# Two chunks of a batch in one load, two tokens in each partition, for two of four batches of an RWKV-5 and squared-ReLU kernel

## The chip, the cores and the metric

The kernel runs on one core of one Trainium2 chip. The core has five queues of instructions that run beside each other: TensorE (PE in the profile; its weight loads are shown as PEld), VectorE (DVE), ScalarE (ACT), GpSimd (POOL) and SyncE (SP), which here only issues transfers. The metric is the device time of one execution in microseconds, taken as the median of several runs.

## The reference

An attention with a decaying state, per batch (4) and head (8, each of 48 columns), over 768 tokens, and then a two-layer network with a squared ReLU over all 3072 tokens:

```
for t in range(S):                       # S = 768
    cur = einsum('bhd,bhe->bhde', u * k[t], v[t])
    y[t] = einsum('bhd,bhde->bhe', r[t], state + cur)
    state = w * state + einsum('bhd,bhe->bhde', k[t], v[t])
x = y.transpose(0, 2, 1, 3).reshape(3072, 384)
h = maximum(x @ w_in, 0)                 # 384 -> 2048
out = (h * h) @ w_out                    # 2048 -> 384
```

r, k and v are float32 arrays of [4, 8, 768, 48], so a token of one head is a run of 192 bytes in memory. w_in and w_out are float32 and are turned to bf16 on the way in.

## The kernel before, in words

**Units.** Tokens are cut into chunks of 128. A unit is one chunk of one batch; there are 24, and unit i is chunk i // 4 of batch i % 4. A unit has 128 tokens in the 128 partitions and all eight heads in the columns. Units 0 to 3 (the first chunks) start from an empty state; each later one needs the state that the unit four before it left.

**Steps of one unit, in the attention.** `ld` loads r, k or v of a unit (L387). `kh` and `rh` scale k and r by powers of w (L424, L430) and write bf16. `T` transposes the scaled pair on PE (L454) and `Tc` copies the result from PSUM to SBUF; for later units `XB`, a transposing transfer, does both. `A` computes the 128 x 128 table of k against r for each head, in eight matmuls (L476). `Bm` multiplies it by a triangular mask on DVE (L501). `Y` multiplies that table by v and adds what the state gives (L509). `U` is the new part of the state, k against v (L536); `S0`, `ts` and `S` decay and sum it. `P0`, `P1`, `du` and `dv` compute the term with u (r times k, times u, summed per head, times v). `vb` turns v to bf16. `xs` adds Y and dv. `X` transposes the sum on PE and `xTc` copies it out; for later units `xX` does it by transfer.

**The network.** Units are put into groups. `F1.g.s` is a piece of the first layer for group g (L587): it fills one PSUM bank with 512 columns. For a group of one unit these are four pieces of 128 hidden columns by 128 tokens, so twelve 128-column matmuls; for a group of two, two pieces by 256 tokens, so six 256-column matmuls. `re` takes the ReLU of the bank (on ACT or DVE) and `sq` squares it. `F2.i.f.4` adds four of sixteen hidden pieces of the second layer for unit i (L615). `os` copies the sum out of PSUM and `out` stores it. The last unit's second layer is done in two column halves (`F2c`).

**Weights.** `lW.0.s` loads a float32 piece of w_in of 384 KB through SP into one of six staging tiles (`st`), and `cW` turns it to bf16 on ACT, DVE or POOL (L403). `W` loads and converts in one transfer issued by POOL (L416), which is done for one piece of w_in and for all four of w_out. A piece of w_in serves two hidden pieces, so F1 step s of a group of two needs piece s, and of a group of one pieces 2s and 2s+1.

**What sets the order.** Nothing is scheduled by the compiler. The string ORDER at the top (L24) lists every step with its engine (P, A, D, G for POOL, S for SP) and its buffers after the slashes: `A.0:P/4/5` is step A of unit 0 on PE into PSUM banks 4 and 5. Each engine runs its steps strictly in that order, so a step that waits holds all that stand behind it on its engine. There are eight PSUM banks; a step that writes one waits until its last reader is done. `Z` steps are matmuls on the identity whose result nobody reads.

**The start.** Small tables come first: w is spread to all partitions by a shuffle (`shw`), u by another (`shu`, L329), then ACT takes logarithms and powers (`logw`, `WkQ`, `WtQ`, `WkS`, `WtS`). u's own load is issued by SP (L323). POOL fills the identity and one mask (L257).

Of the kernel before, what the change touches and what calls it, by code (L numbers as in the profile page):

```python
# [11 lines left out]
ALU = mybir.AluOpType  # L12
# [14 lines left out]
A.0:P/4/5 ld.k.2:S/3 WtS:A P1.3:G kh.1:D/2 lW.0.1:S/0 rh.1:D/2 T.1:P/6 Tc.1:A/1 A.1:P/7/3 Tc.3:A/2 A.3:P/6/2 ld.v.0:S/0  # L27
ld.v.3:S/1 vb.3:G/0 kh.2:D/3 U.3:P/0 du.3:D/1 P0.1:D/2 P1.1:D dv.3:G rh.2:D/3 du.1:D/2 lW.0.5:S/1 cW.0.5:A T.2:P/1 cW.0.1:D
Bm.0.1:D/0 Bm.1.0:D/1 vb.0:A/1 Tc.2:A/3 Bm.0.0:D/2 Y.0:P/5 U.0:P/7 Bm.3.1:D/3 A.2:P/1/4 Bm.3.0:D/4 ld.v.1:S/2 Y.3:P/2 dv.0:G
xs.0:D/0 lW.0.0:S/2 X.0:P/6 cW.0.0:A vb.1:G/2 Bm.1.1:D/5 xs.3:D/1 Y.1:P/5 xTc.0:D/0 X.3:P/3 xTc.3:A/0 P0.2:G/3 P1.2:G  # L30
du.2:D/3 dv.1:G F1.0.0:P/2 re.0.0:A/0 xs.1:D/2 X.1:P/6 lW.0.4:S/3 cW.0.4:G F1.0.2:P/3 re.0.2:A/1 W.0.2:G ld.v.2:S/3 dv.2:G
vb.2:A/3 lW.0.6:S/4 lW.0.7:S/5 Bm.2.0:D/2 W.1.0:G xTc.1:D/1 F1.1.2:P/2 F1.1.0:P/5 Bm.2.1:D/0 Y.2:P/3 re.1.2:A/2 lW.0.3:S/1
wc:S cW.0.6:D U.2:P/1 ld.r.4:S/4 cW.0.7:D F1.1.3:P/6 re.1.0:A/3 sq.1.0:A0/0 re.1.3:A/4 xs.2:D/3 WLcol:A X.2:P/4 xTc.2:D/0
sq.0.0:D2/1 F1.0.3:P/2 cW.0.3:G F1.2.0:P/5 re.0.3:A/5 F1.2.3:P/6 re.2.0:D/3 sq.2.0:A0/2 F1.2.1:P/3 re.2.1:D/0 F1.0.1:P/4
sq.2.1:D2/3 ld.k.4:S/4 WLm:G S0.0:D re.2.3:A/3 sq.2.3:A0/4 S0.2:D F1.2.7:P/2 re.2.7:A/0 W.1.1:G P0.4:D/4 F1.2.6:P/5 kh.4:G/4
F2.3.0.4:P/3 ld.k.5:S/5 F2.0.0.4:P/7 S0.3:D re.2.6:A/3 sq.2.6:A0/5 sq.1.2:D2/6 F1.1.1:P/6 rh.4:D/4 F2.1.0.4:P/1 F1.2.2:P/2
re.2.2:D/3 sq.0.3:A0/7 F1.2.5:P/0 W.1.2:G F2.2.0.4:P/5 re.0.1:D/2 re.1.1:A/5 sq.1.1:A0/8 ld.r.5:S/5 re.2.5:A/5 sq.2.5:A0/9
T.4:P/2 P1.4:D F1.2.4:P/4 Tc.4:A/4 F2.1.4.4:P/1 sq.2.2:D2/10 F2.2.4.4:P/5 U.1:P/6 F2.3.4.4:P/3 rh.5:G/5 kh.5:D/5 T.5:P/0
# [685 lines left out]
```

## Time and profile before

| What | Value |
|---|---|
| median of 3 runs | 173.31 us (173.05 to 173.64) |
| profiled execution | 174.07 us, of which span 172.3 us |
| PE busy | 161.7 us (94%) |
| DVE busy | 139.9 us (81%) |
| ACT busy | 104.5 us (61%) |
| POOL busy | 88.2 us (51%) |
| granted TensorE clock, mean | 0.98 |
| moved by transfers | 29.13 MB in 105,588 packets, 98,008 of them under 512 B |

How to read the profile: the span runs from the first to the last instruction of the profiled execution. Busy time of an engine counts the time in which at least one of its instructions ran; matmuls are pipelined, their ends are modelled, and a busy PE need not be at its peak. In a group of instructions the columns are line, engine, operation, output and inputs by the program's names, shapes and count, then busy time in us and the mean of one instruction in ns, then the idle time of the engine just before them and what ended it. A row of the timeline has start and length in us, and in brackets the idle time before it and the releaser. The chain of waits goes back from the last instruction to what released it; its rows have start, length and what ran. An `x6` is the number of instructions in a row.

### The profile page before, as it was taken

What the parts mean: (1) busy time and instruction counts of PE and PEld (TensorE: products, weight loads), DVE (VectorE), ACT (ScalarE), POOL (GpSimd) and SP (SyncE); (2) the same over time, 40 slices, a digit from 0 to 9 for tenths busy, and PEclk for the clock granted to TensorE, in tenths of its full rate; (3) what the DMA queues carried; (4) which work ended last, traced back from release to release, by engine and by line L of the source; (5) the groups of instructions that cost most, each with busy time, mean ns of one, the idle gap of its engine ahead of it and who ended that gap; (6) DMA issues with size and microseconds to landing.
All of it is one profiled execution on the core that took longest, in us unless ns stands there. A gap on an engine that the chain in (4) does not pass through costs nothing.

```text
span 172.3 us, 4337 instructions
## 1 busy us (share of the span) xinstructions
PE 161.7 (94%) x1691; PEld 121.6 (71%) x1691; DVE 139.9 (81%) x272; ACT 104.5 (61%) x187; POOL 88.2 (51%) x105
## 2 busy tenths in 40 slices
PE   3976899999999997999999999999999999999993
PEld 1445788776787776777687696886686786878772
DVE  5599887569999996788999899779989889682731
ACT  3475477694599485467569276595596454553740
POOL 5425967215857497998339402879922872000000
PEclk9995699999999999999999999999999999999999
DMA  5999999999697998999999997999595963130322
GB/s 99 218 230 257 330 211 192 202 147 224 112 204 153 209 205 190 231 194 183 238 176 211 185 206 140 230 159 234 132 130 107 127 136 98 44 93 0 141 91 91
DMA packets 105588, 29.13 MB, mean 169 GB/s; under 512 B 98008, under 2 KB 105568, under 8 KB 105568
## 3 DMA queue, kind: packets, MB, share of 16 engines
q1 hardware_dynamic: 103672, 26.95, 76.2%
q0 software_dynamic: 1744, 1.77, 6.8%
q8 instruction: 13, 0.21, 0.5%
q10 hardware_dynamic: 152, 0.14, 0.2%
q14 instruction: 7, 0.06, 0.1%
HBM read 20.46 MB, written 4.72 MB: 146 GB/s over the span
## 4 chain that ended last, share of the span: by engine, by line
PE 71%; SPq 10%; DMA 7%; ACT 5%; DVE 2%; issue 2%; POOL 1%; POOLq 0%; ACTq 0%
PE bank L622 31%; PE bank L594 29%; SPq L388 5%; SPq L396 4%; DMA st<-in_moe_w_in_dram 4%; DMA ldv<-in_v_dram 3%; PE bank L494 3%; ACT hr L602 2%; PE bank L531 2%; ACT hq L609 2%; PE bank L527 2%; PE bank L552 2%; PE bank L636 2%; PE bank L578 1%; DVE S0W L567 1%
## 5 line engine op out<-in xcount | busy, mean ns | idle before, releaser
L594 PE MATMUL bank<-xT,W 128*128 128x256 bf16 (+1 forms) x624 | 71.2, 266 | 0.4 <-DVE W L288 0.3
L622 PE MATMUL bank<-W,hq 128*128 128x384 bf16 x368 | 68.5, 326 | 0.3 <-DVE S0W L567 0.3
L594 PEld LDWEIGHTS <-W 128*128 128x128 bf16 x624 | 56.1, 99 | 9.0 <-DVE W L288 0.5
L602 ACT ACTIVATE hr<-bank 128x512 bf16<-128x512 f32 x70 | 40.6, 593 | 27.5 <-PE bank L594 26.8
L609 ACT ACTIVATE hq<-hr 128x512 bf16<-128x512 bf16 x72 | 43.6, 626 | 7.3 <-DVE hr L604 6.1
L622 PEld LDWEIGHTS <-hq 128*128 128x128 bf16 x368 | 33.9, 98 | 19.2 <-ACT hr L602 0.5
L507 DVE TENSOR_TENSOR Bm<-bank,maskJT 128x512 bf16<-128x512 f32 x48 | 31.1, 678 | 0.6 <-PE bank L494 0.6
L604 DVE TENSOR_SCALAR hr<-bank 128x512 bf16<-128x512 f32 x26 | 17.6, 686 | 11.7 <-PE bank L594 9.7
L441 POOL TENSOR_TENSOR P<-P,ub 128x384 f32<-128x384 f32 x14 | 15.0, 1072 | 16.2 <-DVE P L437 15.9
L434 POOL TENSOR_TENSOR rk<-ldr,Wt 128x384 bf16<-128x384 f32 x13 | 13.8, 1063 | 7.8 <-DMA ldr<-in_r_dram 7.8
L449 POOL TENSOR_TENSOR dv<-ldv,du 128x384 f32<-128x384 f32 x16 | 13.9, 878 | 2.8 <-DVE du L444 2.8
L560 DVE TENSOR_TENSOR xs<-bank,dv 128x384 bf16<-128x384 f32 x24 | 13.1, 552 | 2.0 <-PE bank L531 0.9
L444 DVE TENSOR_REDUCE du<-P 128x8 f32<-128x384 f32 x24 | 12.9, 545 | 1.6 <-POOL P L441 1.3
L286 ACT COPY os<-bank 128x384 f32<-128x384 f32 x13 | 5.9, 487 | 13.4 <-PE bank L622 13.4
L573 POOL TENSOR_TENSOR S0W<-ts,WLm 128x384 bf16<-128x384 f32 x9 | 9.4, 1053 | 8.7 <-DVE ts L570 8.6
L428 POOL TENSOR_TENSOR rk<-ldk,Wkhat 128x384 bf16<-128x384 f32 x12 | 12.8, 1076 | 2.0 <-DMA ldk<-in_k_dram 1.9
L531 PE MATMUL bank<-vb,Bm 128*128 128x48 bf16 x192 | 11.6, 187 | 1.5 <-DVE Bm L507 0.9
L613 DVE TENSOR_TENSOR hq<-hr 128x512 bf16<-128x512 bf16 x24 | 12.4, 523 | 0.3
L288 POOL CAST vb<-ldv 128x384 bf16<-128x384 f32 x10 | 6.1, 606 | 12.7 <-DMA ldv<-in_v_dram 11.5
L437 POOL TENSOR_TENSOR P<-ldr,ldk 128x384 f32<-128x384 f32 x10 | 10.6, 1066 | 3.4 <-DMA ldr<-in_r_dram 3.4
L531 PEld LDWEIGHTS <-Bm 128*128 128x128 bf16 x192 | 9.9, 99 | 2.6 <-DVE Bm L507 1.7
L288 DVE COPY os<-bank 128x384 f32<-128x384 f32 (+2 forms) x12 | 6.2, 518 | 6.0 <-PE bank L622 2.7
(67 smaller groups left out, 163.7 us busy)
## 6 DMA issues: line engine op xcount, KB each, us to landing
ldr<-in_r_dram SPq DMA_DIRECT2D x24, 192.0 KB, 4.0
ldk<-in_k_dram SPq DMA_DIRECT2D x24, 192.0 KB, 3.7
ldv<-in_v_dram SPq DMA_DIRECT2D x24, 192.0 KB, 4.2
out_dram<-os SPq DMA_DIRECT2D x23, 192.0 KB, 2.3
st<-in_moe_w_in_dram SPq DMA_DIRECT2D x7, 384.0 KB, 5.6
W<-in_moe_w_out_dram POOLq DMA_DIRECT2D x4, 384.0 KB, 7.2
rkT<-rk SPq DMA_TRANSPOSE x17, 3.7
W<-in_moe_w_in_dram POOLq DMA_DIRECT2D x1, 192.0 KB, 5.1
```

The lines of the kernel that those rows point to most:

```text
L434: e.tensor_mul(scaled("r", i), loaded("r", i), early("WtQ") if i < EARLY else Wt2)
L441: e.tensor_mul(t, t, ub)
L444: e.tensor_reduce(dub[slot[f"dv{i}"]], P0b[slot[f"P{i}"]], axis=mybir.AxisListType.X, op=ALU.add)
L449: e.tensor_mul(dvb[slot[f"dv{i}"]], loaded("v", i), t)
L507: e.tensor_mul(o, a, mask_b)
L531: e.matmul(y[:, hc, D * h : D * (h + 1)], m[h][:, hc, :], vb[:, 2 * hc + h, :], start=(i < B), stop=True, skip_group_check=True,)
L560: e.tensor_add(xsb[slot[f"xs{i}"]].rearrange("p (a b) -> p a b", a=HP), heads(bank(f"bY{i}"), 2 * D), dvb[slot[f"dv{i}"]].rearrange("p (a ...
L594: e.matmul(hp[:, fi, :], W1[f // 2][:, c, 128 * (f % 2) : 128 * (f % 2 + 1)], xt[:, c, :], start=(c == 0), stop=(c == CCH - 1), skip_group ...
L602: e.activation(hr, hp, AF.Relu)
L604: e.tensor_scalar_max(hr, hp, 0.0)
L609: e.activation(hq, hr, AF.Square)
L622: e.matmul(bank(f"bO{i}")[:, 0:d_model], hqb[slot[f"hq{g},{f // m}"]][:, at : at + L], W2[f // 4][:, f % 4, :], start=(summed[i] == 1), st ...
```

## The change

The kernel takes two of the four batches (0 and 1, `DUO = 2`) out of the plain scheme for their first two chunks.

- **Loads.** `ldD.x.p` loads chunks 0 and 1 of batch p, 256 tokens, in one transfer of 384 KB into a staging tile: partition q holds tokens 2q and 2q+1, so a run in memory is two tokens, 384 bytes. Six such loads (k, r, v of two batches) replace twelve loads of 192 KB.
- **Units.** Units 0 and 1 are the even and odd tokens of those 256 of batch 0, units 2 and 3 those of batch 1. Partitions 0 to 63 are chunk 0 and partitions 64 to 127 are chunk 1. Units 4 to 7 are chunks 0 and 1 of batches 2 and 3; from unit 8 on the order is as before.
- **A in quarter tiles.** For the four new units `AD.t` computes the tables of both the even and the odd keys against unit t's queries, each within its own half of the partitions: 32 matmuls of 64 x 64. `BmD` masks them with one of two half masks, which POOL fills at the start (two fills and eight selects more).
- **Y in quarter tiles.** Y of such a unit sums over even and odd keys: 32 small matmuls, and four more that add, for the upper half of the partitions, the state that chunk 0 left. That state comes from new steps: `UC.p` on PE (eight matmuls on the lower half) and `SC.p` on ACT, two copies of 48 x 192 from PSUM into a table `carry`.
- **State.** U of a pair is computed once for 256 tokens (`U.1`, `U.3`, eight matmuls each), and decayed by the square of the old factor (`WL2`). So 18 U steps instead of 20, two of them double.
- **Powers of w.** Four new ones (`WkD`, `WtD`), since neighbouring tokens now differ in partition by a half.
- **Groups.** Twelve groups of two units instead of two groups of one and eleven of two.
- **Where work runs.** u's load moves from SP to POOL; the column of w comes from eight small matmuls (`wc`) instead of two transfers; weight casts move to ACT (6 of 7); seven `Z` steps instead of two; `sq` on DVE 36 instead of 24 times, on ACT 60 instead of 72. Staging tiles: 8 instead of 6.
- **Order.** ORDER is another one throughout. Its start is shown.

```
-GROUPS = [1, 1, 2, 2, 2, 2, 2, 2, 2, 2, 2, 2, 2]
-PAIRED = 0
-EARLY = 4
+GROUPS = [2, 2, 2, 2, 2, 2, 2, 2, 2, 2, 2, 2]
+DUO = 2
+EARLY = 6
...
-w:A ld.r.3:S/0 ld.k.0:S/0 ld.r.0:S/1 shw:D u:S P0.0:G/0 shu:D tab:A logw:A WkQ:A/0 WtQ:A/1 rh.0:D/0 ld.r.1:S/2 ld.k.3:S/1
-WkS:A rh.3:D/1 kh.3:D/1 Z.66.7:P T.3:P/2 ld.r.2:S/3 kh.0:D/0 ld.k.1:S/2 P1.0:G du.0:D/0 P0.3:D/1 T.0:P/3 Tc.0:A/0 Z.22.7:P
...
+ldD.k.0:S/0 w:A tab:A ldD.r.0:S/1 ldD.k.1:S/2 u:G ldD.r.1:S/3 ld.k.4:S/0 shw:D ld.r.4:S/0 logw:A ld.r.5:S/1 WtD.1:A/0
+Z.24.5:P wc:P/2 P0.0:D/0 P0.1:G/1 WtD.0:A/1 rh.1:D/0 ldD.v.1:S/4 WkD.1:A/3 rh.0:D/1 WLcol:A shu:D WkD.0:A/6 kh.3:D/2
+ld.k.5:S/1 WkQ:A/7 P1.1:G kh.1:D/0 rh.3:D/2 ldD.v.0:S/5 Z.34.5:P T.1:P/4 P0.2:G/3 rh.2:D/3 T.3:P/5 P0.3:D/2 lW.0.3:S/6 P1.2:G
+Tc.3:A/0 kh.0:D/1 ld.v.4:S/0 kh.2:D/3 Z.17.2:P T.0:P/3 WtQ:A/0 P1.0:G du.2:D/0 T.2:P/2 kh.4:D/4 Tc.2:A/1 ld.v.5:S/1 P1.3:G
+rh.4:D/4 rh.5:D/5 Z.17.5:P T.4:P/1 Tc.1:A/2 lW.0.6:S/7 du.0:D/1 vb.2:G/0 AD.3:P/5/6 vb.3:G/1 Tc.0:A/3 P0.4:G/4 BmD.3.0:D/0
+Z.3.2:P UC.1:P/0 ld.r.6:S/2 du.3:D/2 SC.1:A Z.6.4:P AD.0:P/2/5 P1.4:G Tc.4:A/4 BmD.3.1:D/1 du.1:D/3 dv.3:G Z.6.0:P Y.3:P/4
+BmD.0.1:D/2 lW.0.5:S/1 P0.5:G/3 A.4:P/6/3 kh.5:D/5 AD.2:P/5/0 Bm.4.1:D/3 lW.0.1:S/0 AD.1:P/1/7 vb.1:G/3 BmD.2.0:D/4 WLm:G
+ld.k.6:S/2 T.5:P/3 BmD.2.1:D/5 vb.4:G/4 Tc.5:A/5 BmD.1.1:D/0 Y.2:P/5 dv.2:G ld.k.13:S/3 BmD.1.0:D/1 vb.0:A/2 dv.0:G xs.3:D/0
+ld.r.9:S/3 cW.0.3:A UC.0:P/3 BmD.0.0:D/4 dv.1:G X.3:P/0 SC.0:A WL2:D lW.0.4:S/3 cW.0.6:A W.0.2:G Y.0:P/7 vb.5:D/5 xs.2:D/1
+WtS:A Y.1:P/1 lW.0.7:S/2 xTc.3:A/0 xs.0:D/2 rh.6:G/6 cW.0.5:A X.2:P/3 ld.k.9:S/4 xs.1:D/3 X.0:P/4 A.5:P/2/5 P1.5:G xTc.0:A/1
+xTc.2:D/0 du.4:D/4 cW.0.1:A ld.r.7:S/4 F1.1.5:P/7 Bm.4.0:D/5 X.1:P/0 ld.k.7:S/5 Bm.5.0:D/4 F1.1.6:P/1 xTc.1:A/1 dv.4:D WkS:A
...
+    mask_half = [const.tile([128, 2, L // 2], BF16, name=f"mask_half_{j}") for j in range(2 if DUO else 0)]
+    for j, m in enumerate(mask_half):
+        nc.gpsimd.memset(m, 1.0)
+        for s in range(2):
+            for p in rows:
+                nc.gpsimd.affine_select(
+                    out=m[p, s, :], in_=m[p, s, :], compare_op=ALU.is_ge, fill=0.0, base=int(s < j) - 1,
+                    pattern=[[1, L // 2]], channel_multiplier=-1,
+                )
...
+        def ldD(e, x, p):
+            t = src[x]
+            a = bass.AP(
+                tensor=t.tensor, offset=t.offset + UNITS[2 * p][0] * H * S * D,
+                ap=[[2 * D, L], [S * D, H], [1, 2 * D]],
+            )
+            e.dma_start(out=staged(f"{x}D{p}").rearrange("p (h x) -> p h x", h=H), in_=a)
...
+        def AD(e, t):
+            for s in (t - t % 2, t - t % 2 + 1):
+                ks, rt = rkTb[slot[f"rkT{s}"]], rkTb[slot[f"rkT{t}"]]
                 for hc in range(HP):
                     for h in range(2):
                         q = slice(64 * h, 64 * h + D)
                         for p in rows:
                             e.matmul(
+                                bank(f"bA{t}{h}").rearrange("p (a s b) -> p a s b", a=HP, s=2)[p, hc, s % 2, :],
+                                ks[q, HP + hc, p], rt[q, hc, p],
                                 start=True, stop=True, skip_group_check=True,
                             )
...
+        def UC(e, p):
+            o = heads(bank(f"bUC{p}"), 2 * D)
             for hc in range(HP):
+                for z in (2 * p, 2 * p + 1):
                     e.matmul(
                         o[:, hc, :],
+                        pair(rk[slot[f"rk{z}"]], 1, hc)[rows[0]],
+                        vbb[slot[f"vb{z}"]][rows[0], 2 * hc : 2 * hc + 2, :].rearrange("p a b -> p (a b)"),
+                        start=(z % 2 == 0), stop=(z % 2 == 1), skip_group_check=True,
                     )
 
+        def SC(e, p):
+            for h in range(2):
+                q = slice(64 * h, 64 * h + D)
+                copy(e, carry[p][q, :, D * h : D * (h + 1)], heads(bank(f"bUC{p}"), 2 * D)[q, :, D * h : D * (h + 1)])
...
+                for hc in range(HP):
+                    e.matmul(
+                        y[rows[1], hc, :], rkTb[slot[f"rkT{i}"]][:, hc, rows[1]], carry[i // 2][:, hc, :],
+                        start=(hc == 0), stop=False, skip_group_check=True,
+                    )
```

More of the change, by code (lines that the diff above doesn't have):

```diff
@@ L12 @@
 ALU = mybir.AluOpType
-GROUPS = [1, 1, 2, 2, 2, 2, 2, 2, 2, 2, 2, 2, 2]
-PAIRED = 0
-EARLY = 4
+GROUPS = [2, 2, 2, 2, 2, 2, 2, 2, 2, 2, 2, 2]
+DUO = 2
+EARLY = 6
 SPREAD = True
 WIDE = ()
-WCP = False
-POOLS = dict(ldr=7, ldk=7, ldv=7, st=6, rk=7, P0=5, dv=5, vb=8, rkT=7, Bm=6, xs=5, hr=6, hq=30, os=4, ts=2, xT1=2, xT2=3)
+WCP = True
+POOLS = dict(ldr=7, ldk=7, ldv=7, st=8, rk=7, P0=5, dv=5, vb=8, rkT=7, Bm=6, xs=5, hr=6, hq=30, os=4, ts=2, xT2=3)
 ORDER = """
-w:A ld.r.3:S/0 ld.k.0:S/0 ld.r.0:S/1 shw:D u:S P0.0:G/0 shu:D tab:A logw:A WkQ:A/0 WtQ:A/1 rh.0:D/0 ld.r.1:S/2 ld.k.3:S/1
```

390 lines of the change are left out of this document (168 added, 222 removed).

## The prediction

> **What bounds the kernel now.** I read the span and the engine shares first, then the busy time by stretches, then the chain of waits for the unit prices on TensorE (PE), and last the timeline of the first 31 us. Columns of the stretches: length, busy time of PE, its weight loads, DVE, ACT and POOL, granted clock, DMA share, GB/s.
>
> ```profile
> span 172.3 us, 4337 instructions
> PE 161.7 (94%) x1691; PEld 121.6 (71%) x1691; DVE 139.9 (81%) x272; ACT 104.5 (61%) x187; POOL 88.2 (51%) x105
> 10.00:15.00 5.00, 2.75 (x42) 1.92 (x41) 4.96 (x11) 2.73 (x4) 1.59 (x3) 0.84 0.91 234
> 15.00:20.00 5.00, 4.29 (x58) 3.59 (x56) 4.55 (x10) 3.51 (x5) 3.84 (x6) 0.50 1.06 293
> 30.25:169.50 139.25, 138.26 (x1432) 104.52 (x1432) 115.89 (x216) 86.76 (x159) 70.34 (x73) 1.00 0.82 160
> 169.50:172.30 2.80, 0.00 (x0) 0.00 (x0) 0.29 (x1) 0.00 (x0) 0.00 (x0) 1.00 0.21 70
> ```
>
> From 30.25 us, where the first second-layer step (F2) runs, to 169.5 us PE is busy 138.26 of 139.25 us. A busy PE need not be PE at its peak, so I count its work by unit prices from the chain:
>
> ```profile
> 25.36 2.65 PE bank L594 x30
> 34.99 0.45 PE bank L464 x8
> 75.01 3.38 PE bank L594 x30
> 78.39 1.30 PE bank L622 x8
> 79.69 0.17 PE bank L552 x4
> 80.00 0.05 PE bank L531 x2
> 80.60 0.65 PE bank L622 x4
> 82.85 0.17 PE bank L578 x3
> 86.64 3.28 PE bank L594 x30
> 89.91 0.55 PE bank L494 x16
> 166.82 2.65 PE bank L636 x32
> ```
>
> One F1 step of a two-unit group (six 256-column matmuls) costs 3.28/5 = 0.655 us; the one-unit groups' 128-column matmuls cost 2.65/30 = 0.088 each, so a pair of their steps takes 24 x 0.088/2 = 1.06 for the same columns as 0.655. F2: 0.65. U: 0.17. X: 0.17. T: 0.45. A: 0.275. F2c: 2.65 in all. Two later Y lie between the end of a U (79.69 + 0.17) and the F2 at 80.60, so one is 0.37. After 30.25 us the written order leaves 83 wide F1 (54.4), one narrow (1.1), 92 F2 (59.8), F2c (2.65), 3 T (1.35), 17 U (2.9), 20 Y (7.4), 20 A (5.5), 10 X (1.7): 136.8. So 2.4 of 139.25 us are gaps: PE bounds everything after 30 us, and this change can move the end only through when PE starts on that work, how much is left then, and new gaps.
>
> **The change, part by part.** *Work that goes.* Twelve groups of two: the 16 narrow F1 steps (8 x 1.06 = 8.5 us) become 8 wide ones (5.2). This takes 3.3 us off PE. But all 84 narrow and 30 wide F1 matmuls that ran before 30.25 us, 84 x 0.088 + 30 x 0.109 = 10.7 us in old prices, now come later.
>
> *What is left at the new start.* In the new order the first F1 (F1.1.5) stands behind four T, all quarter-tile A and Y, X.3, X.2, X.0 and A.5. From it on remain 96 F1 (62.9), 92 F2 (59.8), F2c (2.65), one T (0.45), U.1 and U.3 at double length and 16 others (3.4), 20 Y (7.4), 18 A (4.95), 11 X (1.9): 143.4 us. Call the time of F1.1.5 T0. Span = T0 + 143.4 + gaps + 2.8 of tail. With the old gaps of 2.4, today's 172.3 needs T0 = 23.7. Everything hangs on T0.
>
> *T0, walked through the queues.* The rows:
>
> ```profile
> 2.77 0.82 SPq L324 DMA_DIRECT2D urow<-in_u_dram  x1
> 2.87 0.29 POOL L253 TENSOR_SCALAR_AFFINE_SELECT maskJT<-maskJT 128x128 bf16<-128x128 bf16 x1
> 3.66 0.58 DVE L321 STREAM_SHUFFLE wb<-wrow 128x384 f32<-128x384 f32 x1
> 5.35 0.56 ACT L345 ACTIVATE bank<-logw,cols 128x384 f32<-128x384 f32 x1
> 5.79 0.58 DVE L330 STREAM_SHUFFLE ub<-urow 128x384 f32<-128x384 f32 x1
> 5.94 1.00 POOL L437 TENSOR_TENSOR P<-ldr,ldk 128x384 f32<-128x384 f32 x1 [2.78 <-DMA ldr<-in_r_dram]
> 6.27 1.00 DVE L434 TENSOR_TENSOR rk<-ldr,bank 128x384 bf16<-128x384 f32 x2
> 11.35 1.93 ACT L286 COPY rkT<-bank 128x1024 bf16<-128x1024 bf16 x2 [0.55 <-PE bank L464]
> 13.98 0.51 POOL L288 CAST vb<-ldv 128x384 bf16<-128x384 f32 x1 [3.41 <-DMA ldv<-in_v_dram]
> 14.34 3.07 DVE L507 TENSOR_TENSOR Bm<-bank,maskJT 128x512 bf16<-128x512 f32 x5
> 15.09 0.89 ACT L286 CAST W<-st 128x768 bf16<-128x768 f32 x1 [1.81 <-DMA st<-in_moe_w_in_dram]
> 19.34 1.27 PE L594 MATMUL bank<-xT,W 128*128 128x128 bf16 x12
> L382 POOL COPY WLm<-wcol 48x192 f32<-48x192 f32 x2 | 0.7, 344 | 0.7 <-ACT wcol L377 0.6
> W<-in_moe_w_in_dram POOLq DMA_DIRECT2D x1, 192.0 KB, 5.1
> ```
>
> POOL's preamble ends at 3.17 today (2.87 + 0.30). Two half masks add two fills and eight selects on a quarter of the elements, each select between 0.10 and the full 0.29; I take 0.17. With two index tables that is 1.9 us, so POOL is free at 5.1. Then it issues u, which SP issues today. SP's u took 3.0 us to its use (2.77 to 5.79); POOL's one small weight load took 5.1. So u lands between 8.1 and 10.2; I take 8.2, since it is the same 6 KB transfer.
>
> This is an added wait with a queue behind it: DVE does P0.0 (r0 lands at 5.9: the two 384 KB loads take the place of three 192 KB ones, the third of which released POOL at 5.94) and two rh until 7.3, and then stands at the shuffle of u until 8.2. Behind it are all kh, rh.3, rh.2 and so T and A of every unit; POOL's P1.1 waits for it too. From there DVE runs 0.47 to 0.50 a 384-wide operation (two in 1.00) and 0.61 a Bm (five in 3.07): seven operations to kh.2 end at 12.0. T.2 ends at 12.5; ACT copies Tc.2, Tc.1, Tc.0 at 0.965 each (two in 1.93), with SC.1 and Tc.4 behind, until 17.2. The first quarter-tile A (32 matmuls instead of 8) I price at 0.8, by L531's 0.025 each; bounds are 0.28 (same array work as today's A) and 1.1 (32 x 0.55/16). A quarter-tile Y (32 and 4) is 1.0; bounds 0.4 and 1.4. Then PE: Y.3 to 17.9, A.4, AD.2, AD.1, T.5 to 20.3, and now the chain that decides: Tc.5 (21.4), vb.0 on ACT (21.9), UC.0 on PE (22.2), the weight cast in between on ACT (0.89) and SC.0, two 48x192 copies at 0.35 (23.5), Y.0 (24.5), Y.1 (25.5), X.2, X.0, A.5 (26.2). ACT in parallel: cW.0.6, WtS, xTc.3, cW.0.5 end at 26.4; DVE's xs.1 and xTc.2 end at 26.4. Three queues meet at T0 = 26.5. Today the first F1 starts at 19.34, without the other units being done. Lower bound: DVE alone has 18.0 us of work up to xTc.2 (two shuffles, 24 operations at 0.47, nine Bm at 0.61, two small copies) and starts it at 4.3 (today's 3.66 and an estimated 0.6 for two more casts and three more fills), so 22.3 without any wait; upper bound with u at 10.2 and the dear quarter tiles, 29.
>
> *The loads.* r0 as third of equal loads at 5.94 and v3 seven loads and one weight piece later at 13.98 give 0.95 to 1.0 us per 192 KB; a 384 KB weight piece counts 1.2. A 384 KB two-token load lies between 1.2 and 2.0, I take 1.5. Then piece 5, behind six such loads, seven plain ones and two pieces, lands at 2.9 + 9 + 7 + 3.6 = 22.5. Its cover is ACT, which turns to it at 25.5, so the saved DMA time (6 x 0.5 = 3 us) buys nothing at T0.
>
> *After T0.* Thirty F1 with little F2 between them need two evacuations each:
>
> ```profile
> L609 ACT ACTIVATE hq<-hr 128x512 bf16<-128x512 bf16 x72 | 43.6, 626 | 7.3 <-DVE hr L604 6.1
> L602 ACT ACTIVATE hr<-bank 128x512 bf16<-128x512 f32 x70 | 40.6, 593 | 27.5 <-PE bank L594 26.8
> L286 ACT COPY xT<-bank 128x384 bf16<-128x384 bf16 x6 | 2.8, 483 | 2.6 <-PE bank L578 2.6
> ```
>
> Until F2.4.8.4 PE has 25.9 us. ACT has 20 re (11.9), 15 sq (9.4) and 6.7 of others (four xTc at 0.48, three weight casts, Tc.6, WkS, vb.9), 28 us, of which 2.5 lie before the first re. So PE waits for banks between 0 and 2 us; I take 1.0. F2's weights leave POOL after its some 33 operations from 8.7 us on, at about 41, and are used first at about 53. Costs at nothing: the narrower state updates (covered by PE), WL2 on DVE.
>
> Sum: 26.5 + 143.4 + 2.4 + 1.0 + 2.8 = 176.1 us of span against 172.3, +3.8. The profiled execution took 174.07 with what lies around its span, 0.76 above the median of 173.31 of the runs; added to the median: 177.1 us.
>
> **Rivals.** *Transfers set the start (faster).* If DVE and ACT lose nothing, T0 is piece 5 at 22.5, or 20.7 with the loads at 1.2, plus the cast, but not before DVE's 22.3. At T0 = 22.3 and no new gap the span is 171.0, 172.0 us. The DMA share near 1 from 10 us on speaks for it; DVE at 4.96 of 5 us in the same stretch speaks against. It decides below T0 = 23.1.
> [...]
>
> *No change.* T0 of 23.1 to 24.1: u lands before 7.3 and the quarter tiles cost 0.3. 173.3 us.
>
> *Cold clock (slower still).* The clock was 0.84 and then 0.50 between 10 and 20 us, after PE fell to 2.75 busy of 5 us. From 22.2 to 26.5 the new PE has UC.0, two Y, three X and A.5, about 3 us, and no filler. If the first 3.4 to 6.8 us of F1 run at half clock, 1.7 to 3.4 us are lost: about 179.7 us.
> [...]
> [...]
>
> **How the numbers follow.** Forecast (T0 25 to 28, 175.7 to 179) 0.58; cold clock or late u (above 179) 0.15; a small loss (T0 24.1 to 25, 173.9 to 175.7) 0.10; no change 0.05; transfers 0.12. Measurement tells about 0.3% (0.5 us), so faster 0.12, same 0.05, slower 0.83. Range: from 172.5, which takes in no change, to 180.5; about 0.10 lies below and 0.08 above. Within slower, the likeliest is 175.7 to 179.
>
> **What would show it.** The shuffle of u waiting for a DMA after 7.3 us; first L594-type matmul near 26.5 us with ACT's carry copy and the Y of batch 0 ahead of it in the chain; ACT at the front of the chain from 35 to 50 us; no L594 matmul with 128 columns. The prediction is wrong if F1 starts before 24 us, or if PE's gaps after T0 differ from 3.4 us by more than 2.

## The result, and the profile after

The changed kernel takes 180.8 us (median of four executions, 179.73 to 183.42) against 173.47 us (173.05 to 173.88) for the kernel before: a ratio of 1.040 [1.033, 1.048]. (Here and below a median takes in all executions, a ratio only those within 1.5% of the fastest of their kernel.) Against the 173.31 us on which the forecast stands, that ratio gives 180.3 us: slower, 3.2 us above the forecast of 177.1 and just inside the range to 180.5. The profiled execution took 179.73 us with a span of 178.0, which is 1.9 us above the 176.1 worked out. The four executions differ by the TensorE clock they were granted: spans of 178.0 and 178.4 us at a mean clock of 0.998 and 1.000, 179.8 at 0.981 and 181.7 at 0.962.

The page of the changed kernel, span and engine shares:

```profile
span 178.0 us, 4764 instructions
PE 167.0 (94%) x1885; PEld 124.5 (70%) x1885; DVE 142.3 (80%) x277; ACT 103.3 (58%) x188; POOL 92.9 (52%) x122
```

Its stretches (columns as before: length, PE, weight loads, DVE, ACT, POOL, granted clock, DMA share, GB/s). The later cuts are the first F1, the first F2 and the start of the tail:

```profile
10.00:15.00 5.00, 3.48 (x42) 2.46 (x41) 4.87 (x11) 1.64 (x3) 4.07 (x5) 1.00 1.28 247
15.00:20.00 5.00, 4.94 (x147) 3.55 (x148) 4.77 (x10) 4.21 (x6) 4.92 (x8) 1.00 1.19 278
27.35:54.44 27.09, 26.06 (x328) 22.45 (x328) 26.43 (x49) 23.52 (x44) 18.62 (x21) 1.00 1.10 192
54.44:175.20 120.76, 119.29 (x1148) 88.28 (x1145) 94.29 (x174) 63.58 (x119) 51.80 (x55) 1.00 0.70 143
175.20:178.00 2.80, 0.00 (x0) 0.00 (x0) 0.21 (x1) 0.00 (x0) 0.00 (x0) 0.87 0.27 94
```

After the first F1, PE is busy 26.06 + 119.29 of 147.85 us, so it is still the bound over this stretch as a whole, and the end follows from when that F1 begins and from the 2.50 us in which PE is idle. In the kernel before it began at 19.34 us. The timeline of DVE, POOL and PE in the changed kernel shows where the first 27 us go (start, length, and in brackets the wait):

```profile
3.52 1.08 POOL L263 TENSOR_SCALAR_AFFINE_SELECT mask_half<-mask_half 64x64 bf16<-64x64 bf16 x4
...
10.13 0.01 DVE L323 LOAD_MASK_SELECT ub<-urow  x1 [2.71 <-DMA urow<-in_u_dram]
16.11 0.32 PE L473 MATMUL bank<-rkT,rkT 48*64 48x64 bf16 x16
16.26 0.30 PE L473 MATMUL bank<-rkT 48*64 48x64 bf16 x16
18.68 0.36 PE L509 MATMUL bank<-carry,rkT 128*64 128x96 bf16 x4
18.97 0.69 PE L517 MATMUL bank<-vb,Bm 64*64 64x48 bf16 x32
19.91 0.32 PE L473 MATMUL bank<-rkT 48*64 48x64 bf16 x16
20.25 0.45 PE L473 MATMUL bank<-rkT,rkT 48*64 48x64 bf16 x32
27.35 0.81 PE L585 MATMUL bank<-xT,W 128*128 128x256 bf16 x6
```

DVE stands for 2.71 us until u has come, which POOL issues only when the eight selects are done. The chain of waits shows the load (4.14 us) and then runs through the transposes, the quarter-tile A and Y, and the carry copy:

```profile
5.96 4.14 DMA urow<-in_u_dram
21.48 1.01 ACT rkT L296
22.50 0.41 ACT vb L296
22.91 0.61 ACT W L296
23.54 0.31 ACT carry L296
24.20 0.90 ACT W L296
...
26.12 0.80 ACT W L296
26.96 0.34 DVE xT L298
```

The ACT rows from 24.20 on and the DVE row are the other two queues: DVE and PE arrive at the first F1 at 27.30, ACT at 26.92. From the carry copy on, the chain stays with ACT and then with DVE; PE's own steps to the first F1 (Y.0, Y.1, X.2, X.0, A.5) run beside it.

### The profile page after: what moved, and what is told of

Read it like the earlier page. It is cut to its first block, busy times and chain, and to the rows that moved or that the text cites. A ratio compares the mean times of both kernels' runs of the same rounds, so it can differ in the third digit from the quotient of the medians.

```text
span 178.0 us, 4764 instructions
## 1 busy us (share of the span) xinstructions
PE 167.0 (94%) x1885; PEld 124.5 (70%) x1885; DVE 142.3 (80%) x277; ACT 103.3 (58%) x188; POOL 92.9 (52%) x122
## 4 chain that ended last, share of the span: by engine, by line
PE 77%; DMA 7%; DVE 5%; ACT 5%; POOL 2%; issue 2%; SPq 0%; DVEq 0%; POOLq 0%
PE bank L585 32%; PE bank L613 32%; DMA rkT<-rk 5%; PE bank L665 3%; DMA urow<-in_u_dram 2%; ACT rkT L296 2%; PE bank L530 2%; PE bank L540 2%; PE bank L526 2%; PE bank L627 1%; ACT W L296 1%; DVE dv L446 1%; POOL mask_half L263 1%; PE bank L455 1%; DVE rk L423 1%
## 5 line engine op out<-in xcount | busy, mean ns | idle before, releaser
L585 PE MATMUL bank<-xT,W 128*128 128x256 bf16 x576 | 70.0, 273 | 0.1
L593 ACT ACTIVATE hr<-bank 128x512 bf16<-128x512 f32 x66 | 38.1, 592 | 36.3 <-PE bank L585 34.4
L600 ACT ACTIVATE hq<-hr 128x512 bf16<-128x512 bf16 x60 | 36.4, 627 | 4.1 <-DVE hr L595 3.3
L496 DVE TENSOR_TENSOR Bm<-bank,mask 128x512 bf16<-128x512 f32 x40 | 26.0, 680 | 1.7 <-PE bank L665 1.3
L564 POOL TENSOR_TENSOR S0W<-ts,WLm 128x384 bf16<-128x384 f32 x10 | 10.2, 1022 | 24.0 <-DVE ts L561 12.2
L595 DVE TENSOR_SCALAR hr<-bank 128x512 bf16<-128x512 f32 x30 | 20.0, 684 | 2.4 <-PE bank L585 2.1
L604 DVE TENSOR_TENSOR hq<-hr 128x512 bf16<-128x512 bf16 x36 | 17.6, 499 | 5.2 <-ACT hr L593 4.7
L296 ACT COPY os<-bank 128x384 f32<-128x384 f32 x14 | 6.5, 475 | 17.9 <-PE bank L613 17.2
L446 POOL TENSOR_TENSOR dv<-ldv,du 128x384 f32<-128x384 f32 x13 | 11.2, 861 | 9.8 <-DVE du L441 9.8
L639 PE MATMUL bank<-identity 128*128 128x512 bf16 x24 | 9.2, 526 | 2.9 <-POOL identity masks.py:199 2.9
L431 POOL TENSOR_TENSOR rk<-ldr,Wt 128x384 bf16<-128x384 f32 x10 | 10.8, 1078 | 1.8 <-DMA ldr<-in_r_dram 1.6
L296 ACT COPY rkT<-bank 128x1024 bf16<-128x1024 bf16 x7 | 6.9, 1015 | 7.0 <-PE bank L455 7.0
```

Of the source, the lines that this page charges most:

```text
L296: e.copy(o, a)
L446: e.tensor_mul(dvb[slot[f"dv{i}"]], loaded("v", i), t)
L496: e.tensor_mul(Bmb[slot[f"Bm{i}{h}"]], heads(bank(f"bA{i}{h}"), 128), over(mask, HP))
L585: e.matmul(hp[:, fi, :], W1[f // 2][:, c, 128 * (f % 2) : 128 * (f % 2 + 1)], xt[:, c, :], start=(c == 0), stop=(c == CCH - 1), skip_group ...
L593: e.activation(hr, hp, AF.Relu)
L595: e.tensor_scalar_max(hr, hp, 0.0)
```

## The experiments

All runs are shown together. T0 is the start of the first F1 in the profiled execution and "clock" that execution's mean; the ratio is to the kernel before on the same chip.

| Run | Edit | median us | ratio | span | clock | T0 |
|---|---|---|---|---|---|---|
| e1_u_by_sp | after, u issued by SP | 181.15 | 1.038 [1.030, 1.047] | 179.2 | 0.971 | 27.86 |
| e2_runs_of_192 | after, 192-byte runs | 182.77 | 1.046 [1.037, 1.055] | 180.3 | 0.991 | 29.48 |
| e3_no_late_filler | after, five fillers out | 184.62 | 1.058 [1.050, 1.066] | 182.9 | 0.953 | 30.53 |
| e4_before_u_by_pool | before, u issued by POOL | 174.28 | 1.001 [0.998, 1.005] | 172.4 | 0.978 | 20.01 |
| e5_u_by_sp_filler | e1 and a filler | 181.25 | 1.035 [1.029, 1.042] | 180.2 | 0.981 | 28.46 |
| e6_u_by_sp_half_tiles | e1, half the quarter tiles | 179.12 | 1.025 [1.018, 1.031] | 175.1 | 0.999 | 25.38 |
| e7_before_pairs | before, groups of two only | 177.63 | 1.018 [1.012, 1.023] | 174.7 | 0.970 | 21.81 |
| e8_half_tiles | after, half the quarter tiles | 182.16 | 1.045 [1.040, 1.050] | 180.2 | 0.980 | 28.34 |
| e9_fillers_to_f1 | e5 and three more fillers | 180.08 | 1.031 [1.026, 1.037] | 179.7 | 1.000 | 28.66 |
| e10_before_fillers | before, five fillers | 179.29 | 1.018 [1.011, 1.026] | 176.4 | 0.981 | 23.06 |
| e11_before_fillers2 | e10, other banks | 173.85 | 1.003 [0.999, 1.007] | 171.6 | 1.000 | 19.61 |
| e12_narrow_fillers | e1, fillers in more pieces | 180.20 | 1.031 [1.020, 1.042] | 178.7 | 0.981 | 25.25 |

### u's load back on SP

```
-ldD.k.0:S/0 w:A tab:A ldD.r.0:S/1 ldD.k.1:S/2 u:G ldD.r.1:S/3
+ldD.k.0:S/0 w:A tab:A ldD.r.0:S/1 u:S ldD.k.1:S/2 ldD.r.1:S/3
```

> The changed kernel with one step moved: u's load is issued by SP behind the second two-token load, not by POOL behind its masks. Theory (the wait on u holds DVE, and everything of the start stands behind it): the shuffle of u, which ran at 10.13 us after a wait of 2.71, runs at about 7.4 and waits for nothing; the first F1 comes 1.8 to 2.7 us earlier than its 27.35, so between 24.6 and 25.6, and the span falls by the same, 178.0 to about 175.8. Rival (weights or ACT set the start): the shuffle moves, the first F1 stays within 0.5 us of 27.35.

The wait is gone: the shuffle runs at 7.66 without one, and the first quarter-tile Y begins at 16.23 instead of 18.68. But T0 is 27.86, half a microsecond later than with the late u. Part of PE's timeline:

```profile
7.66 0.58 DVE L323 STREAM_SHUFFLE ub<-urow 128x384 f32<-128x384 f32 x1
16.23 0.36 PE L509 MATMUL bank<-carry,rkT 128*64 128x96 bf16 x4
17.46 0.32 PE L473 MATMUL bank<-rkT 48*64 48x64 bf16 x16
19.05 0.47 PE L473 MATMUL bank<-rkT,rkT 48*64 48x64 bf16 x32 [1.27 <-issue]
27.86 1.46 PE L585 MATMUL bank<-xT,W 128*128 128x256 bf16 x6
```

PE stops for 1.27 us behind the 16th of the 32 matmuls of AD.2, with "issue" as the releaser, so it waits for nothing that the profile shows; and from 19.3 to 29.6 us its clock is 0.5 (six F1 matmuls take 1.46 instead of 0.81). So 2.45 us are won up to 16 us and lost again by 28. The later experiments go after the two suspects, the stop and the clock.

### The runs in memory at 192 bytes again

```
-a = bass.AP(tensor=t.tensor, offset=..., ap=[[2 * D, L], [S * D, H], [1, 2 * D]])
-e.dma_start(out=staged(f"{x}D{p}").rearrange("p (h x) -> p h x", h=H), in_=a)
+for j in range(2):
+    a = bass.AP(tensor=t.tensor, offset=... + D * j, ap=[[2 * D, L], [S * D, H], [1, D]])
+    e.dma_start(out=staged(f"{x}D{p}").rearrange("p (h j d) -> p h j d", h=H, j=2)[:, :, j, :], in_=a)
```

> The changed kernel with each two-token load split into two transfers, the even and the odd tokens, so that runs in memory are 192 bytes again and packets of these loads double; the place in SBUF is the same. Theory (the start hangs on u and the engines' queues, the saved transfer time is covered): first F1 within 0.7 us of 27.35, span within 1 us. Rival (transfers set the start): the pieces land about 3 us later, first F1 near 30, span +2 to +3 us.

T0 is 29.48, 2.1 us later. The chain of waits no longer passes u; it consists of SP's issues and a piece of weights, which lands at 26.70:

```profile
18.39 8.31 DMA st<-in_moe_w_in_dram
...
29.48 0.61 PE bank L586 x2
```

In the changed kernel this piece (6) was issued at 14.35 and landed at 21.05, and ACT turned to it at 24.20, so some 3 us of cover were there. Here it is issued 4.0 us and lands 5.7 us later, which is more than the cover, and ACT waits for it for 1.00 us. So the wide loads do keep the transfers off the path. Two transfers for one also cost two issues on SP, and this run does not part the issues from the width. Nor is it the transfers alone that hold T0: PE stops for 0.73 us behind the 16th matmul of AD.2, as in the first run, its clock is 0.5 from 27.5 to 30.9, and it ends A.5 at 29.40, when ACT ends the cast (29.43).

### Without the fillers behind the first transposes

```
-Z.17.2:P ... Z.17.5:P ... Z.3.2:P ... Z.6.4:P ... Z.6.0:P
```

> The changed kernel without the five filler steps behind the first transposes (13 matmuls on the identity, about 4 us of PE). Theory (the rival of the prediction that the clock falls did not come in the profiled execution because of these fillers): the granted clock goes to 0.5 for 6.8 us somewhere between 13 and 28 us, the first F1 comes 0.5 to 2 us later, the span is 1 to 4 us longer. Against it: the clock stays at 1.0 and the span is the same or 0.3 us shorter, since the fillers stand on PE's path.

The stretches show the price of the clock for this kernel:

```profile
20.00:25.00 5.00, 4.37 (x138) 3.63 (x131) 4.64 (x9) 1.92 (x4) 4.88 (x9) 0.58 0.99 256
25.00:30.00 5.00, 4.71 (x91) 3.89 (x89) 2.84 (x7) 3.85 (x7) 2.70 (x3) 0.50 1.09 227
```

T0 moves from 27.35 to 30.53, the ratio from 1.040 to 1.058 and the median by 3.8 us, although some 3.5 us of filler were taken away in front of it (two of 1.1, one of 0.3, two of 0.5). The mean clock was 0.953 in all four executions. At 0.5 the first F1 step takes 1.46 instead of 0.81 us and the 32 small matmuls of a Y up to 1.05 instead of 0.69, and DVE, busy 5.00 us from 25 to 30 with the fillers, is busy 2.84 without them.

PE stops in this run, too. The five filler steps are 19 matmuls, not 13, and the stop stands 19 matmuls behind the place of the first run: behind the 16 of AD.2 that come first and 19 more.

```profile
20.89 0.46 PE L473 MATMUL bank<-rkT,rkT 48*64 48x64 bf16 x19
21.82 0.38 PE L473 MATMUL bank<-rkT,rkT 48*64 48x64 bf16 x13 [0.46 <-issue]
```

### The kernel before with u on POOL

```
-shw:D u:S P0.0:G/0 shu:D
+shw:D u:G P0.0:G/0 shu:D
```

> The kernel before with u's load issued by POOL instead of SP, nothing else. Theory (a load issued by POOL lands later, 4.1 us after its issue as in the changed kernel): the shuffle runs at about 7.3 us instead of 5.79, DVE's chain shifts by 1.2 to 1.5 us, the span grows by 0.5 to 1.5 us. Rival (the start of this kernel hangs on weight pieces, whose loads now leave SP 0.8 us earlier): span the same or up to 0.8 us shorter.

The shuffle in DVE's timeline:

```profile
6.24 0.01 DVE L330 LOAD_MASK_SELECT ub<-urow  x1 [1.94 <-DMA urow<-in_u_dram]
```

The shuffle moves by only 0.45 us and the time by nothing. So the queue that issues u is not what makes it late. In the changed kernel it is late because POOL has eight selects to do first (free at 5.9, not 3.2) and because the load then takes 4.14 us. What makes it that long is open: it took 3.1 us in this run, and still 3.9 in the run with 192-byte runs, where each load beside it was of 192 KB, so the larger loads are not the reason.

### u by SP, and a filler over the stop

```
-A.4:P/6/3 kh.5:D/5 AD.2:P/5/0
+A.4:P/6/3 kh.5:D/5 Z.24.1:P AD.2:P/5/0
```

> As the run with u's load by SP, and with six wide filler matmuls (1.3 us, 12 instructions) ahead of AD.2. There PE stood at 17.78 us for 1.27 us in the middle of AD.2, waiting for nothing that the profile shows, and the clock then was 0.5 from 19.3 to 29.6 us. Theory (moving u wins about 2.4 us at Y.3, and the stop and the clock gate took it back): with PE busy over that time the clock stays at 1.0, the first F1 comes at 25.5 to 26.3, and the span is 175.8 to 177.0, 1 to 2 us under the changed kernel's 178.0. Rival (the first F1 hangs on weights or ACT's casts): first F1 at 27 or later even at full clock.

The stop at AD.2 is gone, but another of 0.37 us stands in Y.0 (`[0.37 <-issue]` behind its 15th small matmul), and the clock falls at 24.0, for two half-speed F1 steps: T0 28.46. The filler's own 1.4 us came on top. And less had been won before it: the eight wide fillers ahead of the first transposes took 3.60 us where they took 1.90 in the first run, the transposes began at 10.44 instead of 9.20, and at the first quarter-tile Y 1.5 of the 2.45 us were left (17.18 against 18.68).

### u by SP, half of the quarter-tile matmuls

```
-for s in (t - t % 2, t - t % 2 + 1):      # AD: 32 matmuls of 64 queries
+(own keys alone, queries streamed twice)   # AD: 16 matmuls of 128 columns
-for z in both:                             # Y: 32
+for z in (i,):                             # Y: 16
```

> As the run with u's load by SP, with half of the quarter-tile matmuls left out of the four new units: A uses a unit's own keys alone, with the queries streamed twice, so 16 matmuls of twice the length instead of 32, and Y sums over its own keys alone, 16 instead of 32. So part of the attention of these units is left out and A waits for one unit's transposes only. Theory (PE's stop at 17.78 us comes of the many small instructions, 64 in each such A and more in each such Y, which run out faster than the next ones come): no stop of over 0.3 us that nothing visible ends, clock 1.0, first F1 at 24.5 to 25.5, span 174.5 to 176. Rival (the stop has another cause): a stop of about 1.3 us at the same time, clock 0.5 behind it, span as before, 179.

The first F1 in PE's timeline:

```profile
25.38 0.83 PE L586 MATMUL bank<-xT,W 128*128 128x256 bf16 x6 [0.33 <-ACT W L296]
```

With half as many instructions and the same columns in A there is no stop, the clock stays at 1.00, and the profiled execution has a span of 175.1 with T0 at 25.38, 2.0 us before that of the changed kernel. The other executions were at 0.981 to 0.990, and the median of 179.12 holds that in it. Even so, it stays slower than the kernel before, by a ratio of 1.025 [1.018, 1.031].

### The kernel before with groups of two alone

```
-GROUPS = [1, 1, 2, 2, 2, 2, 2, 2, 2, 2, 2, 2, 2]
+GROUPS = [2, 2, 2, 2, 2, 2, 2, 2, 2, 2, 2, 2]
```

The F1, `re` and `sq` steps of the two first groups are joined, and the new first group's F1 starts behind xTc.1. The transposed sums have four buffers, all for groups of two, where the kernel before has two for groups of one and three for groups of two.

> The kernel before with one part of the change alone: units 0 and 1 form one group of two, so all F1 steps are wide; loads, units, A and Y stay. F1 steps of that group stand behind the transpose of unit 1 in the order. Theory (PE bounds all behind the start, a wide step pair saves 3.3 us of PE in all, and the first F1 comes 2.5 us later than 19.34 with some 2 us of narrow work lost there): span 171 to 172.5 against 172.3, so 0 to 1.3 us won. Rival (the early F1 of one unit is worth what it costs, since PE otherwise waits): span 173 to 174.5.

The first F1 in PE's timeline:

```profile
21.81 4.03 PE L593 MATMUL bank<-xT,W 128*128 128x256 bf16 x24 [0.45 <-DVE xT L287]
```

T0 moves from 19.34 to 21.81 and the time by 1.8%. The 3.3 us less of PE work do not show up as a gain. The likely reason is that a group of one unit lets F1 start with one unit done; but the half clock also lasted 10.2 us here and 6.8 in the kernel before, and the run doesn't part the two.

### The late u, half of the quarter-tile matmuls

The same edit as in the half-tile run above, with u still on POOL.

> The changed kernel (u by POOL) with half of the quarter-tile matmuls left out as in the run on u by SP. Theory (the quarter tiles lie on the path between the transposes and the first F1: four A and four Y at about 0.25 and 0.35 saved each): first F1 1 to 2 us earlier than 27.35, span 176 to 177. Rival (DVE and ACT carry the path, the tiles are covered): first F1 within 0.5 us, span 177.5 to 178.

Rows of PE's timeline:

```profile
8.08 0.28 PE L642 MATMUL bank<-identity 128*128 128x128 bf16 x2
11.85 1.17 PE L455 MATMUL bank<-identity,rk 128*128 128x128 bf16 x16 [3.50 <-DVE rk L423]
28.34 1.46 PE L586 MATMUL bank<-xT,W 128*128 128x256 bf16 x6
```

and one of its stretches:

```profile
12.60:16.10 3.50, 3.50 (x25) 2.40 (x23) 3.50 (x8) 1.50 (x2) 3.42 (x4) 0.51 1.22 272
```

T0 is 28.34, later than with all matmuls. In this execution the first eight fillers took 1.90 us and were over at 8.4, PE then stood for 3.5 us until u had come, and the clock was 0.5 from 12.7 to 16.1 and again from 26.3 to 29.8. In the profiled execution of the changed kernel the same fillers ran at half speed (eight in 3.60 us against 1.90; the clock's records begin behind them, at 10.0), lasted to 10.2, and the clock did not fall before the tail. The run can't weigh the quarter tiles; it suggests that what the same wait costs depends on when the clock falls.

### Fillers up to the first F1

```
-A.4:P/6/3 kh.5:D/5 Z.24.1:P AD.2:P/5/0    (from e5)
+A.4:P/6/3 kh.5:D/5 Z.20.1:P AD.2:P/5/0
+Z.4.3:P before UC.0, Z.4.0:P before X.3, Z.8.7:P before Y.0
```

> Theory (the 2.5 us that an earlier u gains up to the first quarter-tile Y are lost again only because TensorE falls silent between 20 and 25 us and its clock drops): with u issued by SP, a filler of 5 wide matmuls before the third quarter-tile A and three short ones (1, 1 and 2 wide matmuls) before the carry matmuls, X.3 and Y.0, the granted clock stays 1.00 from 10 to 30 us, the first F1 begins at 26.0 to 27.0 us and the span is 176 to 177.5, so the ratio to the kernel before is 1.015 to 1.025. Rival (the clock is only a sign; the start is held by DVE and ACT whatever u does): the first F1 begins at 27.4 or later also with the clock at 1.00, and the ratio stays at 1.035 to 1.04.

The clock is 1.00 all the way, and T0 is 28.66, not the 26.0 to 27.0 of the theory. But the run doesn't tell what the clock alone takes. As in the run with one filler, the fillers ahead of the first transposes ran slowly, so that 1.5 of the 2.45 us were left at the first quarter-tile Y (17.17). The nine new fillers then take up to 2.3 us of PE, 1.2 ahead of AD.2 and 1.1 behind it. And the stop is there twice, in PE's timeline:

```profile
19.59 0.28 PE L473 MATMUL bank<-rkT 48*64 48x64 bf16 x11
20.90 0.23 PE L473 MATMUL bank<-rkT 48*64 48x64 bf16 x5 [1.03 <-issue]
25.29 0.37 PE L517 MATMUL bank<-vb,Bm 64*64 64x48 bf16 x12
26.28 0.49 PE L517 MATMUL bank<-vb,Bm 64*64 64x48 bf16 x20 [0.61 <-issue]
```

The places count. Here AD.2 stops behind its 11th matmul, with five fillers (of 512 columns) more ahead than in the first run, where it stopped behind the 16th: the same 16th instruction. Y.0 stops behind its 12th small matmul, with nine fillers more ahead; in the run with one filler step (six matmuls) it stopped behind the 15th: again the same, the 21st without fillers. And from the 16th of AD.2 to the 21st of Y.0 there are 16 + 32 (AD.1) + 8 (T.5) + 36 (Y.2) + 8 (UC.0) + 3 (X.3) + 4 + 21 = 128 matmuls. The page has a queue of transfers of kind "instruction" (packets, MB, share):

```profile
q8 instruction: 15, 0.25, 0.6%
```

Its 15 packets are 0.25 MB, so some 16 KB each. One begins at 18.46 and one at 23.99, and PE goes on 2.4 and 2.3 us later. The count gives the place and not the length: in the run with one filler, the same up to 18.4 us, the transfer of the first of these pieces began at 16.70, and PE passed the place (the 10th matmul of AD.2, at about 19.9) without a stop.

### The kernel before with fillers

```
+Z.16.7:P before A.1, Z.8.0:P before A.3, Z.8.1:P before U.3, Z.4.1:P before T.2, Z.4.5:P before Y.0
```

> The kernel before with five short fillers (4, 2, 2, 1 and 1 wide matmuls on the identity) ahead of A.1, A.3, U.3, T.2 and Y.0, where TensorE stood still for 0.5 to 1.1 us each between 11 and 16.5 us and its clock was then 0.5 from 13.4 to 20.2 us. Theory (the half clock costs the start time in the kernel before too): the clock stays 1.00 up to 20 us, the first F1 begins at 17.3 to 18.6 instead of 19.3, and the span is 170 to 171.5, ratio 0.985 to 0.995. Rival (at that place DVE, at 4.96 of 5 us, sets the start and the clock costs nothing): the first F1 stays at 19.1 to 19.5 and the ratio within 0.997 to 1.003.

Two of the fillers wrote into banks 0 and 1, where the powers of w still lay, so the scaling of unit 2 reads what the fillers left there, and it waited 2.86 us for PE. Its time says nothing on the clock. With the fillers of A.3 and U.3 in banks 6 and 0 instead:

> The kernel before with fillers of 4, 2, 2, 1 and 1 wide matmuls on the identity ahead of A.1, A.3, U.3, T.2 and Y.0, now in PSUM banks that hold nothing then (two fillers of the first try went into banks 0 and 1, where the powers of w lie, and kept the scaling of unit 2 waiting). Theory (the half clock from 13.4 to 20.2 us costs start time in the kernel before too): the clock stays 1.00 up to 20 us, the first F1 begins at 17.3 to 18.8 instead of 19.3, the span is 170 to 171.8, ratio 0.985 to 0.997. Rival (DVE, at 4.96 of 5 us there, sets the start and the clock costs nothing): first F1 at 19.1 to 19.5, ratio 0.997 to 1.003.

A stretch of this last run:

```profile
18.00:20.00 2.00, 1.56 (x29) 1.17 (x26) 2.00 (x6) 0.27 (x1) 2.00 (x4) 1.00 1.12 333
```

The clock is 1.00, DVE is busy 2.00 of 2.00 us, T0 is 19.61 and the time the same. In both kernels the first F1 begins within 0.1 us of the end of DVE's copy xTc.0 (19.56 here, 19.26 in the kernel before). So in the kernel before, the half clock costs nothing that the time shows: DVE sets the start. In the changed kernel it isn't, as the run without fillers showed.

### The same columns in more instructions

```
+if n > 20:          # Z.24.5 and Z.34.5, ahead of the first transposes
+    for _ in range(n):
+        e.matmul(banks[b][:, 0:128], identity, identity, ...)   # 58 narrow ones instead of 16
```

> With u issued by SP, the two fillers ahead of the first transposes are written as 24 and 34 narrow matmuls instead of 6 and 10 instructions, 42 matmuls more on TensorE ahead of everything else and as many columns as before. Theory (the stop in the middle of AD.2 is the end of a 16 KB piece of TensorE's instructions, 128 matmuls after the end of the one before, whatever the work): the stop moves 42 matmuls towards the front, to behind the 14th of the 32 small matmuls of Y.3, or shows as nothing at all, and there is none behind the 16th matmul of AD.2; the next piece ends inside Y.2, behind its 26th small matmul. Rival (the stop belongs to AD.2, its data or its form of matmul): a stop of 1 to 1.3 us stays behind the 16th matmul of AD.2.

This is the test of the count, with the place named ahead. PE's timeline:

```profile
17.36 0.32 PE L473 MATMUL bank<-rkT 48*64 48x64 bf16 x16
17.51 0.43 PE L473 MATMUL bank<-rkT,rkT 48*64 48x64 bf16 x32
19.14 0.90 PE L517 MATMUL bank<-vb,Bm 64*64 64x48 bf16 x26
20.28 0.27 PE L517 MATMUL bank<-vb,Bm 64*64 64x48 bf16 x6 [0.24 <-issue]
25.25 1.46 PE L585 MATMUL bank<-xT,W 128*128 128x256 bf16 x6
```

and the stretch from the first F1 to the first F2:

```profile
25.25:54.86 29.61, 28.47 (x329) 23.81 (x328) 26.54 (x49) 23.43 (x44) 18.08 (x20) 0.92 1.01 199
```

AD.2 runs without a stop, and the only one left is in Y.2, behind the 26th small matmul, as forecast, 2.3 us after a 16 KB instruction transfer began at 18.0. T0 is 25.25, 2.1 us earlier than in the changed kernel, so here, with the pieces of instructions ending elsewhere, u's gain goes through to T0. Against the first run T0 is 2.61 us earlier, and 1.03 of that is the shorter stop; the rest goes with the half clock, which began at 19.3 there and at 23.3 here, and no run shows the one without the other. The half clock lasted until 30.2, and the F1 stage took 29.61 instead of 27.09 us. So the time shows no clear gain: a ratio of 1.031 [1.020, 1.042] against 1.040 [1.033, 1.048]. By an estimate with that stage at 27.09 and the 123.6 us behind it as they were in the changed kernel, the span would be 25.25 + 27.09 + 123.56 = 175.9 us: still 3.6 above the kernel before.

## Why the prediction was right, and where it was off

The direction and the main mechanism held: an added wait for u, a later T0, and PE bound behind it. The size was short, by 1.9 us in the profiled execution and 3.7 in the median (3.2 by the ratio), so the time lies in the class above 179 us, which had a chance of 0.15, and not in the 175.7 to 179 that I held likeliest.

- **Span = T0 + what is left.** This carried the whole case. In all nine variants of the changed kernel that were profiled, from the first F2 to the end takes 123.1 to 123.9 us, and nearly all the difference lies in T0 and in the F1 stage. Against the 23.7 that the old span needed, T0 is 3.65 us late; longer gaps and unit prices add 2.05, which makes up the 5.7 us of span. (In the count of the work, the "16 narrow F1 steps" are 8; their 8.5 us are the price of eight, so the sum stands.)
- **T0: 27.35 for 26.5.** The step that failed is u's landing. I took 8.2, since it was "the same 6 KB transfer"; it was 10.13, close to the upper bound of 10.2. Two terms were short: the selects follow each other at 0.28 us (0.23 of work and 0.05 of issue) where I took 0.17, so POOL issued at 5.96 instead of 5.1; and from there to the landing it took 4.14 instead of 3.0.
- **Quarter tiles.** A was 0.45 us (16.11 to 16.56) against 0.8, Y 1.0 against 1.0. At the end of the first Y I was 1.8 us too early (17.9 for 19.66), mostly through u, and the cheaper AD.2 and AD.1 gave a third of it back by the end of T.5 (21.45 for 20.3).
- **The deciding chain** is the one named up to the carry copy (Tc.5, vb.0, the weight cast). Behind it the chain of waits follows ACT and DVE; PE's way through Y.0, Y.1 and X has hardly a wait, and three queues do meet at T0, within 0.4 us.
- **After T0.** The F1 stage took 27.09 for 26.9. From the first F2 to the tail it took 120.76 for 119.9. PE's idle time after T0 is 2.50 us, 1.5 above the 0.99 of the old stretch, where I had added 1.0. The size of the F1 stage's gap was right (1.03) and its cause wrong: I had ACT short of time for the evacuations, and the chain of waits has no ACT there. The gap is one wait of PE at 33.5 for xs.5, behind dv.5 on DVE (1.33 us where dv.4 took 0.54, and no run shows why):

```profile
31.44 1.33 DVE dv L446
32.90 0.57 DVE xs L548
33.51 0.34 PE bank L569 x3
```

  The unit prices, which by construction needed 1.4 us more in the old kernel, needed 1.95 here. The chain does not pass the first F1 at all: from xTc.2, which ends at 27.30, it stays with DVE, busy 26.43 of the 27.09 us of this stage, up to xs.5. By this chain an earlier T0 with DVE as it is would only have lengthened the wait at 33.5, so DVE's queue belongs in the sum as well.
- **The saved transfer time buys nothing.** Right that it doesn't show at T0, and the cover of 3 us was there. Its size was wrong: without the wide loads a piece of weights lands 5.7 us later, not 3, and with 192-byte runs the transfers became part of the path and T0 2.1 us later.
- **The fourth rival, a cold clock,** happened in the profiled executions of six of the eight variants. Of the 3.4 to 6.8 us at half clock that it was priced at, the kernel before shows the 6.8 (13.41 to 20.24 us) and no row of it the 3.4; the run with the late u and half the tiles has a stretch of that length (12.7 to 16.1). In two of the four executions of the changed kernel, which were not profiled, the mean clock was 0.981 and 0.962, by an estimate 6.8 and 13.8 us at half clock; that could make up the 1.8 and 3.7 us by which their spans exceed 178.0. I had given it 0.15 together with a late u; both came.
- **No change and the faster rival** are ruled out for these variants: T0 never came below 25.2, and the faster one needed less than 23.1.
- **The wide groups** save 3.3 us of PE work and yet, done alone in the kernel before, cost 1.8%: the 2.5 us by which the first F1 came later, and a longer half clock. Whether the changed kernel loses as much by them, no run separates.

What none of my steps had is the stop for instructions. In the changed kernel it costs only 0.19 us (16 of AD.2's matmuls at 19.91, the next at 20.25, where a start-to-start of 0.15 is usual, as from 16.11 to 16.26), because with the late u PE comes to this place 2.45 us later than in the first run, and the transfer of the piece only 1.1 us later (17.6 against 16.5). Together with the half clock behind it, it is what keeps an earlier u from paying.

How far each of u, groups, quarter tiles and clock adds up to the whole 5.7 us of span isn't settled: their effects overlap, and the edits gave between -2.1 and +3.2 us at T0.

## What to carry to other kernels

When one engine is busy from some point to the end, price a change by when that point is reached, and walk all queues to it. Cutting matmuls into quarter tiles multiplies instructions (32 for 8 in A), so count them too: here the 2.45 us that an earlier u gained met a stop of 1.27 us inside a quarter-tile A and some 10 us at half clock, and undoing the late u alone then showed next to nothing (a ratio of 1.038 against 1.040). Before adding fillers, see whether the half clock costs anything: in the kernel before, nothing of its 6.8 us showed (1.003 with the clock at 1.00).

## What the runs showed of the hardware

- **Stops for instructions.** The transfers of kind "instruction" on queue q8 were of some 16 KB (14 packets and 0.23 MB in the changed kernel). In the run with fillers up to the first F1 the two stops of PE without a visible releaser lay 128 matmuls apart, each with its weight load, and the stop moved by the 42 matmuls that the narrow fillers add and by the 19 that the run without the late fillers takes away. That a piece of 16 KB holds 128 matmuls of PE is concluded from these places; no view shows what is in it. PE went on 2.3 to 2.6 us after the transfer of a piece began (17.62 to 20.25 in the changed kernel, 18.01 to 20.28 with the narrow fillers, 18.46 to 20.90 and 23.99 to 26.28 with fillers up to the first F1). The quarter tiles started every 10 to 20 ns (16 of 64 x 64 in 0.15 us, 32 of 64 x 48 in 0.61), so by an estimate 128 of them last 1.2 to 2.4 us, and a piece can be used up before the next is there.
- **The clock.** Half-clock stretches were 3.4 us long (12.7 to 16.1 in the run with the late u and half the tiles), 6.8 (13.41 to 20.24 in the kernel before), 10.2 (the kernel before with groups of two alone) or 13.7 (the run without the late fillers): one to four times 3.41. The clock fell also where PE had been working for most of the time. Stretches of the run with one filler over the stop:

```profile
20.00:22.00 2.00, 1.88 (x100) 1.57 (x90) 1.70 (x3) 0.86 (x1) 2.00 (x3) 1.00 0.91 243
22.00:24.00 2.00, 1.26 (x34) 1.03 (x29) 2.00 (x5) 1.96 (x6) 1.22 (x2) 1.00 1.14 315
24.00:26.00 2.00, 1.63 (x40) 1.34 (x38) 1.14 (x4) 1.98 (x4) 0.65 (x1) 0.51 1.11 183
```

  PE had been busy 1.26 of 2 us before the clock went to 0.51. Over the 3.41 us before it fell, from 20.61, PE was busy for 75%; in the run with fillers up to the first F1 it was busy for 75% from 17.32 to 20.73, and the clock stayed at 1.00. So in these two runs the busy share alone doesn't tell when it falls. What makes it fall, no run shows.
- **A POOL select of 64 x 64 took 0.23 us in the changed kernel, one of 128 x 128 0.29:** a quarter of the elements, four fifths of the time.
